# A mixture-of-experts stage whose first layer keeps the expert's weights in the array and streams the tokens, with the second layer's weights resident

## The chip, the cores and the metric

The kernel runs on one core of one Trainium2 chip. The metric is device time in microseconds (us) of one execution; the profile is one execution recorded by the hardware profiler. TensorE appears in it twice, as PE (matmuls) and PEld (weight loads), VectorE as DVE, ScalarE as ACT, GpSimd as POOL and SyncE as SP; SPq, POOLq and PEldq are the instruction queues of these engines.

## The reference

Everything is float32. A block-sparse attention over 4 batches, 8 heads, 768 positions and 64 dimensions per head gives `x` of 3072 tokens by 512. A gate picks one of 8 experts for each token, and the token goes through that expert's two layers:

```python
logits = x @ w_gate                      # 3072 x 8
expert_idx = np.argmax(logits, axis=1)
gate_w = softmax(logits)[arange, expert_idx]
for e in range(8):                       # the tokens of expert e
    h = np.maximum(x_e @ w1[e], 0.0)     # 512 -> 1024
    y_e = h @ w2[e]                      # 1024 -> 512
out = gate_w[:, None] * y
```

Each expert's `w1` is 512x1024 and its `w2` 1024x512, 2 MB either way.

## The kernel before, in words

The kernel has three stages.

**Attention** (to about 426 us): for 16 pairs of heads and two halves of the queries, scores with keys on the partitions (`scores`, L187), their exponential on ACT, the product with V (`attend`, L208), and `rows_out` (L223), which turns the result into rows of tokens, sums the exponentials and computes the gate's logits. `rows_out` issues on TensorE, back to back, six small float32 products with a moving operand of one column (L231) and three with one of 144 columns (L236); a float32 product is two weight loads and two matmuls in the trace, so that these show as 12 and 6. The rows go to a scratch tensor `x_rows` in HBM. During this stage the POOL queue loads all eight experts' `w1` into one resident tile, 16 MB (`load_w`, L92).

**Routing** (to about 460 us): DVE computes for every token its expert and its slot, so that the tokens stand sorted by expert in 31 chunks of 128 slots, a chunk having one expert only. `xe` (L458) holds the expert of each chunk; `g_idx` and `s_idx` (L495, L498) hold the rows to gather and to scatter.

**Experts** (from about 464 us): 31 chunks. For chunk i

- `gather(i)` (L510): POOL gathers 128 rows of `x_rows` by an indirect DMA into `xg` (four buffers).
- `fetch(i)` (L517): SP reads the chunk's expert from `xe` into a register and fetches that expert's `w2`, 2 MB, into one of two buffers.
- `turn_x(i)` (L522): four transposes on TensorE put the features on the partitions (`tpg`), and DVE copies them to `xgT` (two buffers).
- `layer1(i)` (L529): `xgT` is the weight operand, 128 columns at a time, and the resident `w1` streams through the array 512 columns at a time: 8 matmuls into `hp`, 128 tokens by 1024 features. DVE and ACT apply the ReLU on a half each (L540, L541) and write `h`.
- `turn_h(i)` (L543): `h` has the tokens on the partitions, so eight more transposes (`tph`) and two copies (DVE L550, ACT L552) give `hT`.
- `layer2(i)` (L554): `hT` is the weight operand and the fetched `w2` streams, 8 matmuls of 512 columns into `zp`. DVE multiplies by the gate's weight (L559) and POOL scatters the rows into the output (L560).

The loop at the end of the function writes this with layer 1 one chunk ahead of layer 2. A scheduler turns it into one instruction list per engine, each run in order, and puts the semaphores in. It also pulls reads of `xe` into registers ahead of other work. Every float32 matmul below is two weight loads and two matmuls in the trace; a transpose is one of each.

Of the kernel before, what the change touches and what calls it, by code (L numbers as in the profile page):

```python
# [8 lines left out]
F32 = mybir.dt.float32  # L9
# [3 lines left out]
AF = mybir.ActivationFunctionType  # L13
# [5 lines left out]
def kernel(  # L19
# [11 lines left out]
    nc = tc.nc  # L31
    P = 128
# [7 lines left out]
    N, DM = out.shape  # L40
    E = moe_w_gate.shape[1]
    F = moe_w1.shape[2]
    DB = DM // P
    FB = F // P
    NT = N // P
    NC = NT + E - 1
# [7 lines left out]
    big = ctx.enter_context(tc.tile_pool(name="big", bufs=1))  # L54

    ident = const.tile([P, P], F32, name="ident")
# [2 lines left out]
    nc.scalar.dma_start(wg[:], moe_w_gate.rearrange("(c p) e -> p c e", p=P))  # L59
    lgn = const.tile([P, NT, E], F32, name="lgn")  # L60
    lmax = const.tile([P, NT], F32, name="lmax")
    w1_all = big.tile([P, DB, E, F], F32, name="w1_all")

    x_d = nc.dram_tensor("x_rows", (N, XW), F32, kind="Internal").ap()

# [24 lines left out]
        loaded[(b, pr)] = got  # L90

    def load_w(e):  # L92
        nc.gpsimd.dma_start(w1_all[:, :, e, :], moe_w1[e].rearrange("(c p) f -> p c f", p=P))

    load(0, 0)

# [194 lines left out]
    for i in range(len(steps) + 2):  # L291
        if i < len(steps):
            n, half, g = steps[i]
            if half == 1 and g == 0 and n + 2 < len(pairs):
                load(*pairs[n + 2])
            if half == 0 and g == 2 and n % 2 == 0 and n // 2 < E:
                load_w(n // 2)
            for c in range(g * GR, (g + 1) * GR):
                scores(n, half, c)
        if 0 <= i - 1 < len(steps):  # L300
            n, half, g = steps[i - 1]
            for c in range(g * GR, (g + 1) * GR):
                attend(n, half, c)

        if i < len(steps) and steps[i][2] == 1:
            n, half, _ = steps[i]
            turning = turn(*pairs[n + 1], half) if n + 1 < len(pairs) else iter(())
            next(turning, None)
            if i > 3:
                rows_out(*steps[i - 2][:2])  # L310
            for _ in turning:
                pass
# [75 lines left out]
    xe = const.tile([1, NC], I32, name="xe")  # L388
# [113 lines left out]
    xp = ctx.enter_context(tc.tile_pool(name="xp", bufs=2))  # L502
    wp = ctx.enter_context(tc.tile_pool(name="wp", bufs=2))
    ps_h = ctx.enter_context(tc.tile_pool(name="ps_h", bufs=2, space=PSUM))
    ps_m = ctx.enter_context(tc.tile_pool(name="ps_m", bufs=2, space=PSUM))
    ps_z = ctx.enter_context(tc.tile_pool(name="ps_z", bufs=2, space=PSUM))
    w2v = moe_w2.rearrange("e (a p) d -> p e a d", p=P)
    st = [{} for _ in range(NC)]

    def gather(i):  # L510
        xg = st[i]["xg"] = xp.tile([P, XW], F32, name="xg", bufs=4)
        nc.gpsimd.indirect_dma_start(  # L512
            out=xg[:], out_offset=None, in_=x_d[:, :],
            in_offset=bass.IndirectOffsetOnAxis(ap=g_idx[:, i : i + 1], axis=0),
        )

    def fetch(i):  # L517
        e = nc.sync.value_load(xe[0:1, i : i + 1], min_val=0, max_val=E - 1)
        w2 = st[i]["w2"] = wp.tile([P, FB, DM], F32, name="w2")
        nc.sync.dma_start(w2[:], w2v[:, bass.ds(e, 1)].rearrange("p e a d -> p (e a) d"))  # L520

    def turn_x(i):  # L522
        tp = ps_m.tile([P, DB, P], F32, name="tpg", tag="m")
        for c in range(DB):
            nc.tensor.transpose(tp[:, c, :], st[i]["xg"][:, c * P : (c + 1) * P], ident[:])
        st[i]["xT"] = xp.tile([P, DB, P], F32, name="xgT")
        nc.vector.tensor_copy(st[i]["xT"][:], tp[:])  # L527

    def layer1(i):  # L529
        e = nc.tensor.value_load(xe[0:1, i : i + 1], min_val=0, max_val=E - 1)  # L530
        hp = ps_h.tile([P, 2, 512], F32, name="hp")
        h = st[i]["h"] = xp.tile([P, F], F32, name="h")
        for f in range(2):
            for c in range(DB):
                nc.tensor.matmul(  # L535
                    hp[:, f, :], lhsT=st[i]["xT"][:, c, :],
                    rhs=w1_all[:, c, bass.ds(e, 1), f * 512 : (f + 1) * 512].rearrange("p e f -> p (e f)"),
                    start=(c == 0), stop=(c == DB - 1),
                )
        nc.vector.tensor_relu(h[:, :512], hp[:, 0, :])  # L540
        nc.scalar.activation(h[:, 512:], hp[:, 1, :], AF.Relu)  # L541

    def turn_h(i):  # L543
        hT = st[i]["hT"] = xp.tile([P, FB, P], F32, name="hT")
        for g in range(2):
            tp = ps_m.tile([P, 4, P], F32, name="tph", tag="m")
            for m in range(4):
                nc.tensor.transpose(tp[:, m, :], st[i]["h"][:, (4 * g + m) * P : (4 * g + m + 1) * P], ident[:])  # L548
            if g == 0:
                nc.vector.tensor_copy(hT[:, :4, :], tp[:])  # L550
            else:
                nc.scalar.copy(hT[:, 4:, :], tp[:])  # L552

    def layer2(i):  # L554
        zp = ps_z.tile([P, DM], F32, name="zp")
        for fb in range(FB):
            nc.tensor.matmul(zp[:], lhsT=st[i]["hT"][:, fb, :], rhs=st[i]["w2"][:, fb, :], start=(fb == 0), stop=(fb == FB - 1))  # L557
        zo = xp.tile([P, DM], F32, name="zo")
        nc.vector.tensor_scalar(zo[:], zp[:], scalar1=st[i]["xg"][:, DM : DM + 1], scalar2=None, op0=ALU.mult)  # L559
        ins = nc.gpsimd.indirect_dma_start(  # L560
            out=out[:, :], out_offset=bass.IndirectOffsetOnAxis(ap=s_idx[:, i : i + 1], axis=0),
            in_=zo[:], in_offset=None, bounds_check=N - 1, oob_is_err=False,
        )
        ins = getattr(ins, "ins", ins)
        tc.declare_no_dep(ins, group="rows_out", reason="disjoint rows")
        tc.add_to_no_dep_group("rows_out", ins)
        st[i].clear()

    for i in range(2):
        gather(i)  # L570
        fetch(i)
    turn_x(0)
    layer1(0)
    for i in range(NC):
        if i + 2 < NC:
            gather(i + 2)
        if i + 1 < NC:
            turn_x(i + 1)
            layer1(i + 1)
        turn_h(i)  # L580
        layer2(i)
        if i + 2 < NC:
            fetch(i + 2)


# [28 lines left out]
```

## Time and profile before

| what | us |
|---|---|
| median of 3 runs | 968.87 (968.75 to 971.04) |
| the profiled execution's own time | 969.39 |
| its span, first to last instruction | 967.7 |
| attention, to the last work of L236 | about 426 |
| first matmul of layer 1 | 466.45 |
| one chunk in the loop | 15.88 |
| last scatter issued | 960.06 |

The span leaves out 1.7 us of the execution's own time. The profile's table of busy time gives each engine's share of the span; the timeline lists instructions in order of time, merged, with the start and the length of each piece; the table by stretches gives the busy time and the granted clock between two instants.

### The profile page before, as it was taken

How to read it: one execution, taken by the hardware profiler on the slowest of the kernel's cores; microseconds unless marked ns; L12 is line 12 of the kernel's file. 1: busy time of each engine (PE TensorE's matmuls, PEld its weight loads, DVE VectorE, ACT ScalarE, POOL GpSimd, SP SyncE). 2: the span in 40 equal slices, each digit the busy share in tenths (PEclk: the TensorE clock that was granted, in tenths of full speed). 3: DMA queues.
4: the chain of work that ended last, by engine and by line, in shares of the span. 5: the costliest groups of instructions: out<-in, count | busy, mean ns of one | idle time of the engine just before them, and what ended most of it. 6: DMA issues, size and time to landing. Idle time of an engine off the chain costs nothing.

```text
span 967.7 us, 10826 instructions
## 1 busy us (share of the span) xinstructions
PE 901.3 (93%) x4110; PEld 458.7 (47%) x4110; DVE 321.4 (33%) x621; ACT 221.5 (23%) x323; POOL 76.4 (8%) x103
## 2 busy tenths in 40 slices
PE   4999999999999999964799999999999999999996
PEld 2455555555555555534344444444444444444442
DVE  3555555555555555544111111111111111111111
ACT  1444444444444444420000000000000000000000
POOL 4000000000000000000111101010101010101000
PEclk9999999999999999985899999999999999999999
DMA  9982222222222210004136354544445454535350
GB/s 307 391 243 66 66 65 57 62 66 67 66 66 66 67 50 17 17 21 175 44 117 210 123 188 136 182 145 174 156 171 166 157 178 149 186 140 199 128 177 0
DMA packets 112255, 122.41 MB, mean 126 GB/s; under 512 B 56451, under 2 KB 72835, under 8 KB 112196
## 3 DMA queue, kind: packets, MB, share of 16 engines
q1 hardware_dynamic: 102484, 90.28, 30.8%
q0 software_dynamic: 9184, 31.33, 8.3%
q8 instruction: 36, 0.59, 0.2%
q14 instruction: 23, 0.19, 0.1%
q10 hardware_dynamic: 528, 0.02, 0.0%
HBM read 108.93 MB, written 14.52 MB: 128 GB/s over the span
## 4 chain that ended last, share of the span: by engine, by line
issue 47%; POOL 5%; PE 1%; DVE 1%; POOLq 0%; DVEq 0%
POOL xg L512 3%; POOL out_dram L560 1%; PE tok_ps L492 1%; DVE oh_r L487 0%; POOLq L609 0%; DVE oh_c L479 0%; DVE oh_c L483 0%; POOLq L512 0%; DVE sl L467 0%; POOLq L560 0%; DVE pr__10054 L432 0%; PE cps L437 0%; PE cps L438 0%; POOL lt_strict L409 0%; DVE xk L452 0%
## 5 line engine op out<-in xcount | busy, mean ns | idle before, releaser
L535 PE MATMUL hp<-w_all,xgT 128*128 x496 | 221.8, 600 | 16.5 <-DVE xgT L527 16.5
L557 PE MATMUL zp<-w,hT 128*128 128x512 f32 x496 | 218.2, 593 | 1.1 <-DVE hT L550 1.1
L200 ACT ACTIVATE e<-s 128x768 f32<-128x768 f32 x192 | 155.3, 811 | 94.8 <-PE s L198 93.1
L195 PE MATMUL s<-qT,kT 64*128 64x384 f32 x768 | 167.4, 514 | 0.0
L535 PEld LDWEIGHTS hp<-w_all,xgT 128*128 128x128 f32 x496 | 92.3, 191 | 128.2 <-issue 104.8
L206 DVE TENSOR_TENSOR esum<-esum,e 128x768 f32<-128x768 f32 x128 | 122.6, 958 | 71.5 <-ACT e L200 64.5
L215 PE MATMUL op<-e,v_sb 128*64 128x384 f32 x768 | 144.8, 499 | 0.0
L557 PEld LDWEIGHTS zp<-w,hT 128*128 128x128 f32 x496 | 91.8, 190 | 105.3 <-issue 103.8
L552 ACT COPY hT<-tph 128x512 f32<-128x512 f32 x31 | 18.1, 585 | 436.8 <-PE tph L548 436.8
L195 PEld LDWEIGHTS s<-qT,kT 64*128 64x128 f32 x768 | 64.1, 188 | 64.8 <-ACT e L200 38.0
L559 DVE TENSOR_SCALAR zo<-zp,xg 128x512 f32<-128x512 f32 x31 | 23.3, 751 | 204.3 <-PE zp L557 204.3
L540 DVE TENSOR_SCALAR h<-hp 128x512 f32<-128x512 f32 x31 | 21.4, 692 | 207.5 <-PE hp L535 207.5
L215 PEld LDWEIGHTS op<-e,v_sb 128*64 128x64 f32 x768 | 46.6, 136 | 80.1 <-issue 79.9
L560 POOL DMA_INDIRECT out_dram<-zo,s_idx x31 | 31.5, 1017 | 429.7 <-DVE zo L559 429.7
L198 PE MATMUL s<-pen,oh 64*128 64x384 bf16 x384 | 63.8, 326 | 0.0
L206 DVE TENSOR_TENSOR esum<-e 128x768 f32<-128x768 f32 x32 | 30.7, 958 | 68.4 <-ACT e L200 68.4
L231 PEld LDWEIGHTS xr<-ones,esum 128*128 128x128 f32 x384 | 45.4, 192 | 1.8 <-DVE esum L206 1.2
L231 PE MATMUL xr<-ones,esum 128*128 128x1 f32 x384 | 45.0, 244 | 0.0
L548 PEld LDWEIGHTS tph<-ident,h 128*128 128x128 f32 x248 | 30.0, 141 | 16.4 <-issue 16.4
L548 PE MATMUL tph<-ident,h 128*128 128x128 f32 x248 | 36.9, 273 | 0.0
L396 POOL IOTA first_w_i<- 128x8 int32 x1 | 0.1, 134 | 421.7 <-SPq L372 421.7
L512 POOL DMA_INDIRECT xg<-x_rows,g_idx x31 | 30.3, 977 | 31.9 <-issue 31.9
(116 smaller groups left out, 400.3 us busy)
## 6 DMA issues: line engine op xcount, KB each, us to landing
w<-in_moe_w_dram SPq DMA_DIRECT2D x31, 2048.0 KB, 10.3
w_all<-in_moe_w_dram POOLq DMA_DIRECT2D x8, 2048.0 KB, 32.9
k_sb<-in_k_dram SPq DMA_DIRECT2D x32, 192.0 KB, 3.7
q_sb<-in_q_dram SPq DMA_DIRECT2D x32, 192.0 KB, 3.3
v_sb<-in_v_dram SPq DMA_DIRECT2D x16, 384.0 KB, 3.3
x_rows<-xb SPq DMA_DIRECT2D x16, 384.0 KB, 3.8
xg<-x_rows,g_idx POOLq DMA_INDIRECT x31, 7.3
out_dram<-zo,s_idx POOLq DMA_INDIRECT x31, 7.7
```

The lines of the kernel that those rows point to most:

```text
L195: nc.tensor.matmul(s[:, hh, :CW], lhsT=kT[r, c * P : (c + 1) * P], rhs=qT[r, cols], start=True, stop=False)
L198: nc.tensor.matmul(s[:, hh, :CW], lhsT=oh[r, c, :], rhs=pen[r, cols], start=False, stop=True)
L200: nc.scalar.activation(e[:], s[:, :, :CW], AF.Exp, scale=scale)
L206: nc.vector.tensor_add(t[:], es[(n, half, 0)][:] if c == 1 else t[:], e[:])
L215: nc.tensor.matmul(op[hh * D : (hh + 1) * D, :], lhsT=v_sb[:, hh, c, :], rhs=e[:, hh, :], start=(c == 0), stop=(c == NCH - 1),)
L231: nc.tensor.matmul(xr[:, HC * M + 2 * m + hh : HC * M + 2 * m + hh + 1], lhsT=esum[:, hh, m * P : (m + 1) * P], rhs=ones[:], start=True, s ...
L512: nc.gpsimd.indirect_dma_start(out=xg[:], out_offset=None, in_=x_d[:, :], in_offset=bass.IndirectOffsetOnAxis(ap=g_idx[:, i : i + 1], axis=0),
L535: nc.tensor.matmul(hp[:, f, :], lhsT=st[i]["xT"][:, c, :], rhs=w1_all[:, c, bass.ds(e, 1), f * 512 : (f + 1) * 512].rearrange("p e f -> p ...
L548: nc.tensor.transpose(tp[:, m, :], st[i]["h"][:, (4 * g + m) * P : (4 * g + m + 1) * P], ident[:])
L557: nc.tensor.matmul(zp[:], lhsT=st[i]["hT"][:, fb, :], rhs=st[i]["w2"][:, fb, :], start=(fb == 0), stop=(fb == FB - 1))
L559: nc.vector.tensor_scalar(zo[:], zp[:], scalar1=st[i]["xg"][:, DM : DM + 1], scalar2=None, op0=ALU.mult)
L560: ins = nc.gpsimd.indirect_dma_start(out=out[:, :], out_offset=bass.IndirectOffsetOnAxis(ap=s_idx[:, i : i + 1], axis=0), in_=zo[:], in_of ...
```

## The change

The two layers change roles. `w2` of all experts is now the resident tile `w2_all`, and the chunk's `w1` is what SP fetches. In layer 1 a 128x128 block of `w1` is the weight operand and the chunk's 128 tokens (`xgT`) stream: 32 matmuls of 128 columns in place of 8 of 512. The result has the features on the partitions already, so `turn_h` with its eight transposes and two copies goes, and the ReLUs write `hT` directly. Layer 2 is as before except that its moving operand comes from the resident tile, at an address from a register. In the loop, `fetch` is written ahead of layer 1 where it stood behind layer 2.

```diff
-    w1_all = big.tile([P, DB, E, F], F32, name="w1_all")
+    w2_all = big.tile([P, FB, E, DM], F32, name="w2_all")
...
-        nc.gpsimd.dma_start(w1_all[:, :, e, :], moe_w1[e].rearrange("(c p) f -> p c f", p=P))
+        nc.gpsimd.dma_start(w2_all[:, :, e, :], moe_w2[e].rearrange("(a p) d -> p a d", p=P))
...
-        w2 = st[i]["w2"] = wp.tile([P, FB, DM], F32, name="w2")
-        nc.sync.dma_start(w2[:], w2v[:, bass.ds(e, 1)].rearrange("p e a d -> p (e a) d"))
+        w1 = st[i]["w1"] = wp.tile([P, DB, F], F32, name="w1")
+        nc.sync.dma_start(w1[:], w1v[:, bass.ds(e, 1)].rearrange("p e c f -> p (e c) f"))
...
     def layer1(i):
-        e = nc.tensor.value_load(xe[0:1, i : i + 1], min_val=0, max_val=E - 1)
-        hp = ps_h.tile([P, 2, 512], F32, name="hp")
-        h = st[i]["h"] = xp.tile([P, F], F32, name="h")
-        for f in range(2):
-            for c in range(DB):
-                nc.tensor.matmul(
-                    hp[:, f, :], lhsT=st[i]["xT"][:, c, :],
-                    rhs=w1_all[:, c, bass.ds(e, 1), f * 512 : (f + 1) * 512].rearrange("p e f -> p (e f)"),
-                    start=(c == 0), stop=(c == DB - 1),
-                )
-        nc.vector.tensor_relu(h[:, :512], hp[:, 0, :])
-        nc.scalar.activation(h[:, 512:], hp[:, 1, :], AF.Relu)
-
-    def turn_h(i):
         hT = st[i]["hT"] = xp.tile([P, FB, P], F32, name="hT")
         for g in range(2):
-            tp = ps_m.tile([P, 4, P], F32, name="tph", tag="m")
-            for m in range(4):
-                nc.tensor.transpose(tp[:, m, :], st[i]["h"][:, (4 * g + m) * P : (4 * g + m + 1) * P], ident[:])
+            hp = ps_h.tile([P, FB // 2, P], F32, name="hp")
+            for m in range(FB // 2):
+                fb = g * (FB // 2) + m
+                for c in range(DB):
+                    nc.tensor.matmul(
+                        hp[:, m, :], lhsT=st[i]["w1"][:, c, fb * P : (fb + 1) * P], rhs=st[i]["xT"][:, c, :],
+                        start=(c == 0), stop=(c == DB - 1),
+                    )
             if g == 0:
-                nc.vector.tensor_copy(hT[:, :4, :], tp[:])
+                nc.vector.tensor_relu(hT[:, : FB // 2, :], hp[:])
             else:
-                nc.scalar.copy(hT[:, 4:, :], tp[:])
+                nc.scalar.activation(hT[:, FB // 2 :, :], hp[:], AF.Relu)
...
     def layer2(i):
+        e = nc.tensor.value_load(xe[0:1, i : i + 1], min_val=0, max_val=E - 1)
         zp = ps_z.tile([P, DM], F32, name="zp")
         for fb in range(FB):
-            nc.tensor.matmul(zp[:], lhsT=st[i]["hT"][:, fb, :], rhs=st[i]["w2"][:, fb, :], start=(fb == 0), stop=(fb == FB - 1))
+            nc.tensor.matmul(
+                zp[:], lhsT=st[i]["hT"][:, fb, :], rhs=w2_all[:, fb, bass.ds(e, 1), :].rearrange("p e d -> p (e d)"),
+                start=(fb == 0), stop=(fb == FB - 1),
+            )
...
     for i in range(2):
-        gather(i)
         fetch(i)
+        gather(i)
...
         if i + 2 < NC:
             gather(i + 2)
+            fetch(i + 2)
         if i + 1 < NC:
             turn_x(i + 1)
             layer1(i + 1)
-        turn_h(i)
         layer2(i)
-        if i + 2 < NC:
-            fetch(i + 2)
```

On TensorE, in the middle of the loop, the list before reads as follows (`zp` is layer 2 of a chunk, `tpg` the turned tokens of the next, `tph` the turned hidden features, `hp` layer 1; ISA sets an address from a register):

```order
L557 MATMUL zp<-w_11692,hT 128x512 x8
L525 MATMUL tpg<-ident,xg 128x128 x4
L548 MATMUL tph<-ident,h 128x128 x4
L535 ISA
L535 MATMUL hp<-w_all,xgT 128x512
```

The last two rows come eight times in all; then follow the other four `tph` and the next eight `zp`. With the change the same place reads:

```order
L526 MATMUL tpg<-ident,xg 128x128 x4
L551 ISA
L551 MATMUL zp<-w_all,hT 128x512
L551 ISA
L551 MATMUL zp<-w_all,hT 128x512
L538 MATMUL hp<-xgT,w_11505 128x128 x32
L551 ISA
L551 MATMUL zp<-w_all,hT 128x512
```

The `tph` are gone, the 32 `hp` stand in one run, and two of a chunk's eight `zp` have moved between the turned tokens and layer 1, which needs them. That is so in 20 chunks; in the last 7 of the loop one `zp` stands there, behind a read of `xe`.

On SP, at the end of the routing, the list before has each of the first two fetches right behind its own read of `xe`:

```order
L518 TENSOR_LOAD xe
L518 ISA x2
L520 ISA
L520 DMA w_10155<-in_moe_w_dram 128x8x512
L518 TENSOR_LOAD xe
L518 ISA x2
L520 ISA
L520 DMA w_10168<-in_moe_w_dram 128x8x512
```

With the change 17 such reads come first, of which the last is the first row here:

```order
L519 TENSOR_LOAD xe
L519 ISA x2
L521 ISA
L521 DMA w_10153<-in_moe_w_dram 128x4x1024
L521 ISA
L521 DMA w_10166<-in_moe_w_dram 128x4x1024
```

So the first fetch has moved behind 16 further reads. The fetches bring 1024 contiguous numbers per run where they brought 512.

On TensorE, at the start of the experts, the tokens of four chunks are turned ahead of the first layer 1, where before it were two chunks (one row of `tpg`, x8), with reads of `xe` behind them:

```order
L548 ISA x2
L526 MATMUL tpg<-ident,xg 128x128 x16
L548 TENSOR_LOAD xe
L548 ISA x2
L548 TENSOR_LOAD xe
```

There are five reads behind the 16 transposes, then `hp` of chunks 0 and 1 (x32 each), `zp` of chunk 0, `hp` of chunk 2, and so on.

## Rows read from the trace of the kernel before

**Rows 1.** The page's busy time of each engine: us, share of the span, instructions.
```profile
PE 901.3 (93%) x4110; PEld 458.7 (47%) x4110; DVE 321.4 (33%) x621; ACT 221.5 (23%) x323; POOL 76.4 (8%) x103
```

**Rows 2.** Busy time by stretches: stretch, length, engines, granted clock, DMA share, GB/s.
```profile
443.00:457.00 14.00, 9.17 (x43) 9.17 (x44) 5.99 (x11) 0.00 (x0) 0.00 (x0) 0.50 0.84 299
462.00:468.00 6.00, 3.54 (x10) 2.30 (x11) 1.38 (x2) 0.00 (x0) 2.67 (x3) 0.50 0.64 178
507.17:523.05 15.88, 15.31 (x44) 7.32 (x44) 2.63 (x5) 1.08 (x2) 1.99 (x3) 1.00 0.49 163
523.05:538.93 15.88, 15.31 (x44) 7.32 (x44) 2.64 (x5) 1.08 (x2) 2.00 (x3) 1.00 0.49 167
```

**Rows 3.** Timeline of TensorE over one chunk: start, length, engine, line, instruction, count.
```profile
641.63 7.03 PE L557 MATMUL zp<-w,hT 128*128 128x512 f32 x16
648.50 0.60 PE L525 MATMUL tpg<-ident,xg 128*128 128x128 f32 x4
648.94 0.60 PE L548 MATMUL tph<-ident,h 128*128 128x128 f32 x4
650.11 7.13 PE L535 MATMUL hp<-w_all,xgT 128*128 x16 [0.57 <-DVE xgT L527]
657.08 0.60 PE L548 MATMUL tph<-ident,h 128*128 128x128 f32 x4
657.51 0.59 PE L557 MATMUL zp<-w,hT 128*128 128x512 f32 x1
```

**Rows 4.** Timeline of VectorE over the same place.
```profile
648.71 0.75 DVE L559 TENSOR_SCALAR zo<-zp,xg 128x512 f32<-128x512 f32 x1 [6.54 <-PE zp L557]
649.37 0.68 DVE L527 COPY xgT<-tpg 128x512 f32<-128x512 f32 x1
```

**Rows 5.** Timeline of matmuls and weight loads in `rows_out`; two rows cut to an instant.
```profile
416.83 1.50 PE L231 MATMUL xr<-ones,esum 128*128 128x1 f32 x12
418.19 0.98 PE L236 MATMUL xr<-mix,oT 128*128 128x144 f32 x6
...
416.83 1.42 PEld L231 LDWEIGHTS xr<-ones,esum 128*128 128x128 f32 x12 [0.60 <-DVE esum L206]
418.16 0.79 PEld L236 LDWEIGHTS xr<-mix,oT 128*128 128x128 f32 x6
...
418.40 0.53 PE L236 MATMUL xr<-mix,oT 128*128 128x144 f32 x3
...
418.89 0.29 PE L236 MATMUL xr<-mix,oT 128*128 128x144 f32 x1
```

**Rows 6.** Durations in ns (min/median/max) of weight loads in `rows_out`.
```profile
L231 PEld LDWEIGHTS xr<-ones,esum x12: 186/192/192, 416.8 to 418.1; 128*128 128x128 f32 x12
L236 PEld LDWEIGHTS xr<-mix,oT x6: 190/190/192, 418.2 to 418.8; 128*128 128x128 f32 x6
```

**Rows 7.** Timeline of TensorE: eight transposes in a row, and the routing's matmuls.
```profile
447.83 10.44 PE L492 MATMUL tok_ps<-oh_c,oh_r 128*128 128x31 f32 x48 [8.38 <-DVE oh_r L487]
...
950.26 1.04 PE L548 MATMUL tph<-ident,h 128*128 128x128 f32 x8
```

**Rows 8.** SP's reads of `xe`, durations in ns, first and last start; its first fetches.
```profile
L518 SPq TENSOR_LOAD <-xe x31: 262/262/284, 442.2 to 460.5; - x31
...
L518 SPq TENSOR_LOAD <-xe x3: 267/274/275, 444.7 to 445.9; - x3
...
L520 SPq DMA_DIRECT2D w<-in_moe_w_dram x2: 380/392/405, 443.1 to 444.3; - x2
...
DMA to landing us min/median/max: 14.1/14.1/14.1
```

**Rows 9.** Timeline of the experts' start: POOL's gathers, TensorE.
```profile
460.42 1.06 POOL L512 DMA_INDIRECT xg<-x_rows,g_idx  x1 [22.75 <-issue]
464.33 0.95 POOL L512 DMA_INDIRECT xg<-x_rows,g_idx  x1 [0.30 <-issue]
...
464.14 1.08 PE L525 MATMUL tpg<-ident,xg 128*128 128x128 f32 x4 [5.87 <-DMA xg<-x_rows,g_idx]
465.54 1.12 PE L525 MATMUL tpg<-ident,xg 128*128 128x128 f32 x4 [0.31 <-DMA xg<-x_rows,g_idx]
466.45 14.88 PE L535 MATMUL hp<-w_all,xgT 128*128 x32
```

**Rows 10.** The page's DMA issues: count, KB each, median us to landing.
```profile
w<-in_moe_w_dram SPq DMA_DIRECT2D x31, 2048.0 KB, 10.3
w_all<-in_moe_w_dram POOLq DMA_DIRECT2D x8, 2048.0 KB, 32.9
xg<-x_rows,g_idx POOLq DMA_INDIRECT x31, 7.3
```

**Rows 11.** Timeline of the end.
```profile
951.86 7.13 PE L557 MATMUL zp<-w,hT 128*128 128x512 f32 x16 [0.57 <-DVE hT L550]
...
960.06 0.98 POOL L560 DMA_INDIRECT out_dram<-zo,s_idx  x1 [7.58 <-DVE zo L559]
```

More of the change, by code (lines that the diff above doesn't have):

```diff
@@ L506 @@
     ps_z = ctx.enter_context(tc.tile_pool(name="ps_z", bufs=2, space=PSUM))
-    w2v = moe_w2.rearrange("e (a p) d -> p e a d", p=P)
+    w1v = moe_w1.rearrange("e (c p) f -> p e c f", p=P)
     st = [{} for _ in range(NC)]
@@ L569 @@
     for i in range(2):
+        fetch(i)
         gather(i)
-        fetch(i)
     turn_x(0)
```

## The prediction

> **What bounds the kernel now.** First the busy times of the page [rows 1]: TensorE works 93% of the span, every other compute engine a third or less. Then the table by stretches [rows 2]: two chunks of the expert stage, 15.88 us each, have TensorE busy 15.31 us at full granted clock, DVE 2.6 us, ACT 1.1 us and the DMA engines half their time. So a chunk costs what TensorE's list for it costs, and the timeline of TensorE over one chunk [rows 3] gives the parts by their starts: layer 2 6.87 us (641.63 to 648.50; 16 matmuls, 0.429 each), turned tokens 0.44, the first four `tph` with the wait behind them 1.17 (648.94 to 650.11), layer 1 6.97, the other four `tph` 0.43. These make 15.88. The wait is for DVE, which must finish `zo` before it copies the turned tokens [rows 4]: from the first transpose at 648.50 to layer 1 at 650.11 pass 1.61 us.
>
> **What goes.** The `tph` with the wait, 1.17 + 0.43 = 1.60 us a chunk. Two copies of `hT` go too, but DVE and ACT are idle most of the chunk [rows 2], so that is worth nothing by itself. The wait for DVE stays possible, but the list now has two `zp` (1.72 us) in 20 chunks between the turned tokens and layer 1: 0.44 + 1.72 is over 1.61, so no wait. In seven chunks only one `zp` stands there: 0.44 + 0.86 = 1.30, a wait of 0.31 each, 2.2 us in all.
>
> **What is added.** Layer 1 streams as many columns as before (8 x 512 = 32 x 128), but in 64 matmuls a chunk with a weight load each, where 16 had one each. At 0.429 us for 512 columns, 128 take 0.107; what the pair of load and matmul costs is the whole question. No row shows this pair, its neighbours do [rows 5, 6]:
>
> - 12 pairs with one moving column, so weight loads and little else: 1.42 us less the last load's 0.19, over 11 steps, 0.112 a pair.
> - 6 pairs with 144 columns: from the second matmul (418.40) to the last (418.89) 4 steps of 0.1225. The stream alone is 0.429 x 144 / 512 = 0.121. A weight load that takes about 0.11 therefore lies wholly beside the matmul ahead of it.
> - 8 transposes, 128 columns each: 1.04 less 0.27 over 7 steps, 0.110 a pair [rows 7].
> - At half the granted clock, the routing's 48 pairs with 31 columns: 10.44 less 0.40 over 47 steps, 0.214, twice the 0.107 of the load, with nothing on top for the columns [rows 2, 7].
>
> So the pair costs the longer of load and stream, 0.112 against 0.107. I take 0.112, the row nearest in its load; 0.110 and 0.1225 bound it. Layer 1 then costs 64 x 0.112 = 7.17 us a chunk, 0.20 more than its 6.97.
>
> The register addresses move from layer 1's operand to layer 2's, eight settings a chunk; layer 1 had them without a gap, so I count nothing.
>
> **The fetches.** Per chunk the bytes are the same. Written earlier, `fetch(i+2)` waits only for the buffer that layer 1 of chunk i reads, and has until layer 1 of i+2, two chunks less one layer 1: 2 x 14.5 - 7.2 = 21.8 us, against a landing of 10.3, at most 14.1 where two start together [rows 8, 10]. Gathers and scatters keep their order on POOL. SP has nothing else queued behind a waiting fetch but the next fetch. The resident load becomes 16 MB in runs half as long; an expert's lands in 32.9 us [rows 10], some 400 us ahead of its use, so I count nothing.
>
> **The start of the experts pays.** SP now does 17 reads of `xe` ahead of the first fetch. 28 steps from 444.7 to 460.5 are 0.564 us each [rows 8], so the first fetch goes out at 442.2 + 17 x 0.564 + 0.3 = 452.1 in place of 443.1. Two fetches took 14.1 us to land, so 466.2 without company; the four gathers, issued from 460.42 to 465.28 [rows 9], now share the DMA engines with them (the fetches moved 4.2 MB at 299 GB/s, the gathers 1.07 MB [rows 2]), which puts all of it at about 469. TensorE's list turns four chunks, not two, ahead of the first layer 1, so it waits for the fourth gather too, whose issue ends at 465.28 and which in any case lands 2.6 us later (as the first did: 461.48 to 464.14), 467.9. With 0.9 us for the last transposes at the low clock, and five reads of `xe` behind them (five times some 0.56 us, hidden if the queue runs ahead), layer 1 of chunk 0 starts between 468.8 and 473; I take 471, against 466.45 before.
>
> **The sum.** From there TensorE is one list: layer 1 31 x 7.17 = 222.2; layer 2 31 x 16 x 0.429 = 213.0 (rounded up by the 0.0004 that 6.87/16 has more); turned tokens 27 x 0.44 = 11.9; the waits 2.2; the edges between blocks 1.5 (half of the 0.10 that layer 1 shows before, 31 times); the low clock at the start 1.0 (32 matmuls took 14.88 where 31 x 0.429 + 0.59 = 13.9 was due [rows 3, 9]). Together 451.8, so the last `zp` ends at 922.8. The end is unchanged: from the last `zp` (951.86 + 16 x 0.429 = 958.73 [rows 11]) to the end of the span at 967.70 are 8.97 us. The span is then 931.8, the execution's own time 1.7 more, 933.5. The profiled execution, at 969.39, is 0.5 above the median of 968.87, so I predict **933.0 us** beside that median, 3.7% faster.
>
> **Where the skill speaks.** The Trainium skill, page "TensorE: Matmul & The Clock Gate", section on the back-to-back issue gap, says that in a stream of weight load and matmul pairs a 128-column matmul takes about 81 ns where the isolated one takes 56. Carried over as an estimate, these 25 ns on each of 1984 pairs of 0.107 would give 0.132 and about 973 us, no gain at all. The 144-column pairs at 0.1225, 2 ns above their stream, speak against it.
>
> **The rivals.**
>
> 1. *The pairs cost more than their longer half.* A step between streams, not seen at 512 columns because it hides there, or a TensorE queue that cannot issue 128 instructions in 7 us. The six 144-column pairs, taken from the very first (418.19 to 418.89, 5 steps), cost 0.14 each, since the first stands 0.21 ahead of the second. If every pair paid that, 1984 x 0.028 = 56 us more: 989 us, slower. It decides at a pair of 0.130, where 1984 x 0.018 eats the whole gain. Against it: the four even steps. If only each of the eight chains of eight matmuls paid 0.1 us once, 25 us: 958, still faster.
> 2. *Load and stream run one after the other* because each load must wait for the array to be free of the matmul ahead. A pair is then 0.112 + 0.107 = 0.22 and the time 933 + 1984 x 0.107 = 1145 us. Against it speak both the 144-column steps and the 48 routing pairs. The same page of the Trainium skill, in its part on row and column tiling, says that a load overlaps matmuls in flight only where it targets other rows of the array; all loads here use all rows, so by that rule this is the case. The trace disagrees, at 0.1225 a pair.
> 3. *The weights come late.* If the first fetch, or the gathers beside it, takes longer than reckoned, the start moves by up to 10 us: 943. If fetches took over 21.8 us in the loop, every chunk would wait; the longest shown is 14.1.
>
> **How the numbers follow.** A measurement of this kernel tells a change of about 0.3%, some 3 us, from none. The forecast, pairs between 0.110 and 0.1225 and a start between 468.8 and 473, spans 933 - 4 - 2 - 1.5 = 925 to 933 + 21 + 2 = 956; I give it 0.89, rival 3 within it. A pair at the bare 0.107 would save 10, 923: 0.03 for that or less. Rival 1 has 0.05, with 0.02 of it near no change; rival 2 0.03. Faster 0.92, same 0.02, slower 0.06. The upper end, with every pair as slow as one of 144 columns, is the least likely part of the forecast, so the range is 922 to 952.
>
> **What would show it.** Right: layer 1 of a chunk in one run of 64 matmuls over 7.0 to 7.4 us, no idle time between two blocks in most chunks, a chunk of 14.5 us, a first layer 1 near 471 at 452 for the first fetch, TensorE still at full granted clock. Wrong: a pair of 0.13 or more in the timeline of layer 1; gaps ahead of `hp` that end with a DMA; a granted clock below 1 in the loop.

## The result, and the profile after

The changed kernel takes 935.79 us (median of 4 runs, 933.29 to 943.27) against 968.83 of the kernel before in the same series: a ratio of 0.967, 95% interval 0.961 to 0.973. The prediction was 933.0 in a range of 922 to 952.

The execution shown here took 937.63 us, its span is 935.9. The page's busy times, to set beside [rows 1]:

```profile
PE 881.2 (94%) x5350; PEld 562.5 (60%) x5350; DVE 303.1 (32%) x590; ACT 206.4 (22%) x292; POOL 78.0 (8%) x103
```

TensorE has 1240 matmuls more and is busy 20 us less. The timeline of TensorE over two chunks of the loop (start, length, engine, line, instruction, count), which answers to [rows 3]:

```profile
646.64 0.60 PE L526 MATMUL tpg<-ident,xg 128*128 128x128 f32 x4
647.08 1.88 PE L551 MATMUL zp<-w_all,hT 128*128 x4
648.80 7.31 PE L538 MATMUL hp<-xgT,w 128*128 128x128 f32 x64
655.94 5.32 PE L551 MATMUL zp<-w_all,hT 128*128 x12
661.09 0.60 PE L526 MATMUL tpg<-ident,xg 128*128 128x128 f32 x4
```

A chunk lasts 14.45 us (646.64 to 661.09) instead of 15.88, and no row shows idle time ahead of it. Layer 1 takes 7.14 us from its start to that of the next block, 0.1116 us for each of the 64 pairs of weight load and matmul; layer 2 keeps 0.429 a matmul. In a chunk with only one `zp` ahead of layer 1 the wait for the turned tokens is there:

```profile
894.39 0.60 PE L526 MATMUL tpg<-ident,xg 128*128 128x128 f32 x4
894.82 1.02 PE L551 MATMUL zp<-w_all,hT 128*128 x2
895.99 7.41 PE L538 MATMUL hp<-xgT,w 128*128 128x128 f32 x64
```

The one `zp` (two matmuls) takes 0.86 us from 894.82, so TensorE is free for layer 1 at 895.68; it starts at 895.99, 0.31 later. The stretches (length, PE, PEld, DVE, ACT, POOL, granted clock, DMA share, GB/s) show TensorE without a gap at full clock; beside it the DMA engines are half idle, as in [rows 2]:

```profile
600.00:700.00 100.00, 100.00 (x587) 73.51 (x586) 14.27 (x21) 4.04 (x7) 13.96 (x14) 1.00 0.51 180
700.00:800.00 100.00, 100.00 (x583) 73.19 (x582) 14.27 (x21) 3.73 (x7) 13.96 (x14) 1.00 0.52 184
```

The start of the experts is another matter. TensorE, to set beside [rows 7, 9] (`issue` marks idle time in which the engine waited for nothing that the profile shows):

```profile
451.39 10.44 PE L492 MATMUL tok_ps<-oh_c,oh_r 128*128 128x31 f32 x48 [8.38 <-DVE oh_r L487]
470.65 1.08 PE L526 MATMUL tpg<-ident,xg 128*128 128x128 f32 x4 [8.82 <-DMA xg<-x_rows,g_idx]
...
475.34 1.09 PE L526 MATMUL tpg<-ident,xg 128*128 128x128 f32 x4 [0.81 <-DMA xg<-x_rows,g_idx]
478.91 13.36 PE L538 MATMUL hp<-xgT,w 128*128 128x128 f32 x92 [2.49 <-issue]
```

The routing's matmuls stand 3.56 us later than before, and from them to the first layer 1 pass 27.5 us where before it was 18.6. SP's instructions of the fetch's line (durations in ns, first and last start), the wait that ends among them (us in total, times, longest) and the landing of the first two fetches show what held them:

```profile
L521 SPq EVENT_SEMAPHORE  x35: 17/17/6946, 455.5 to 874.2; - x35
L521 SPq FUSED_REGOPS  x31: 37/37/48, 455.4 to 874.1; - x31
L521 SPq MOVE w<-in_moe_w_dram x31: 29/29/39, 462.8 to 874.2; - x31
...
SPq L521 <- DVE s_idx L498: 7.0, 1, 7.0
...
DMA to landing us min/median/max: 15.4/15.4/15.4
```

SP had its 17 reads behind it at 455.4 and then stood 6.9 us waiting for the routing's last instruction on DVE (`s_idx`, L498); the first fetch went out at 462.8 and landed 15.4 us later, at 478.2, where layer 1 starts at 478.91. The page's DMA issues (KB each, median us to landing), beside [rows 10]:

```profile
w<-in_moe_w_dram SPq DMA_DIRECT2D x31, 2048.0 KB, 7.8
w_all<-in_moe_w_dram POOLq DMA_DIRECT2D x8, 2048.0 KB, 31.0
...
xg<-x_rows,g_idx POOLq DMA_INDIRECT x31, 3.4
```

The sum of the profiled execution: from the first layer 1 to the last scatter it has 453.30 us (478.91 to 932.21) instead of 493.61, 40.3 less; the start is 12.5 later (478.91 against 466.45); behind the last scatter the span goes on 3.69 us instead of 7.64, 4.0 less. Together 31.8, which is 967.7 less 935.9.

### The profile page after: what moved, and what is told of

The parts are those of the page before. It is cut to its first block, busy times and chain, and to the rows that moved or that the text cites. A ratio compares the mean times of both kernels' runs of the same rounds, so it can differ in the third digit from the quotient of the medians.

```text
span 935.9 us, 13135 instructions
## 1 busy us (share of the span) xinstructions
PE 881.2 (94%) x5350; PEld 562.5 (60%) x5350; DVE 303.1 (32%) x590; ACT 206.4 (22%) x292; POOL 78.0 (8%) x103
## 4 chain that ended last, share of the span: by engine, by line
issue 46%; POOL 5%; PE 1%; DVE 1%; POOLq 0%; DVEq 0%
POOL xg L512 3%; POOL out_dram L557 1%; PE tok_ps L492 1%; DVE oh_r L487 0%; POOLq L604 0%; DVE oh_c L479 0%; DVE oh_c L483 0%; DVE sl L467 0%; POOLq L512 0%; POOLq L557 0%; DVE pr__10054 L432 0%; PE cps L437 0%; PE cps L438 0%; POOL lt_strict L409 0%; DVE xk L452 0%
## 5 line engine op out<-in xcount | busy, mean ns | idle before, releaser
L538 PEld LDWEIGHTS hp<-xgT,w 128*128 128x128 f32 x1984 | 228.4, 194 | 20.2 <-DVE xgT L528 11.6
L538 PE MATMUL hp<-xgT,w 128*128 128x128 f32 x1984 | 230.0, 277 | 3.5 <-issue 2.5
L551 PE MATMUL zp<-w_all,hT 128*128 x496 | 222.3, 592 | 0.0
L551 PEld LDWEIGHTS zp<-w_all,hT 128*128 128x128 f32 x496 | 89.8, 190 | 91.3 <-issue 91.3
L545 ACT ACTIVATE hT<-hp 128x512 f32<-128x512 f32 x31 | 18.5, 597 | 468.3 <-PE hp L538 461.8
L543 DVE TENSOR_SCALAR hT<-hp 128x512 f32<-128x512 f32 x31 | 21.4, 691 | 137.3 <-issue 117.0
L198 PEld LDWEIGHTS <-oh 64*128 64x128 bf16 x384 | 19.6, 95 | 25.6 <-issue 1.7
L526 PEld LDWEIGHTS tpg<-ident,xg 128*128 128x128 f32 x124 | 16.4, 151 | 25.7 <-issue 25.0
```

Of the source, the lines that this page charges most:

```text
L198: nc.tensor.matmul(s[:, hh, :CW], lhsT=oh[r, c, :], rhs=pen[r, cols], start=False, stop=True)
L538: nc.tensor.matmul(hp[:, m, :], lhsT=st[i]["w1"][:, c, fb * P : (fb + 1) * P], rhs=st[i]["xT"][:, c, :], start=(c == 0), stop=(c == DB - 1),)
L543: nc.vector.tensor_relu(hT[:, : FB // 2, :], hp[:])
L551: nc.tensor.matmul(zp[:], lhsT=st[i]["hT"][:, fb, :], rhs=w2_all[:, fb, bass.ds(e, 1), :].rearrange("p e d -> p (e d)"), start=(fb == 0), ...
```

## The experiments

In the loop the question was what a pair of load and stream costs and what the transposes and their wait were worth; ahead of it, why the start was late; and behind it, why the end was early. The kernel before had medians of 969.6, 969.8 and 969.7 us in the three series, so that times can be set side by side.

### Layer 1 in 64 columns

```diff
-                for c in range(DB):
-                    nc.tensor.matmul(
-                        hp[:, m, :], lhsT=st[i]["w1"][:, c, fb * P : (fb + 1) * P], rhs=st[i]["xT"][:, c, :],
...
+                for t in range(2):
+                    cols = slice(t * P // 2, (t + 1) * P // 2)
+                    for c in range(DB):
+                        nc.tensor.matmul(
+                            hp[:, m, cols], lhsT=st[i]["w1"][:, c, fb * P : (fb + 1) * P], rhs=st[i]["xT"][:, c, cols],
...
```

> The changed kernel with layer 1's moving tile halved: 64 token columns stream through each weight tile, twice, so a chunk has 128 float32 pairs of a 128-column weight load and a 64-column matmul instead of 64 pairs of 128 columns. Theory, that the weight load sets a pair's pace (0.1116 us each in the changed kernel's trace, whatever streams beside it): layer 1 takes 128 x 0.112 = 14.3 us a chunk, 7.15 more, times 31 chunks = 222 us, so about 1158 us. Rival A, that the stream sets it (0.107 for 128 columns, half of that for 64): a pair takes about 0.056, layer 1 stays at 7.1 us and the time at about 936. Rival B, that load and stream run one after the other (0.11 and half a stream): about 0.165 a pair, 21 us a chunk, about 1370 us.

Measured: 1184.64 us (one run). TensorE's timeline in the loop:

```profile
716.83 14.40 PE L540 MATMUL hp<-xgT,w 128*128 128x64 f32 x128
731.06 5.37 PE L553 MATMUL zp<-w_all,hT 128*128 x12
```

128 pairs take 14.23 us, 0.1112 each: with half the stream a pair costs what it did. The weight load sets the pace, and both rivals fall. The total is 27 us above the theory's 1158, and 25 of them are the clock. TensorE at the experts' start:

```profile
479.23 54.84 PE L540 MATMUL hp<-xgT,w 128*128 128x64 f32 x256 [2.48 <-issue]
533.86 9.05 PE L553 MATMUL zp<-w_all,hT 128*128 x16
542.75 14.40 PE L540 MATMUL hp<-xgT,w 128*128 128x64 f32 x128
```

and the stretches there (the last number but two is the granted clock):

```profile
480.00:500.00 20.00, 20.00 (x96) 20.00 (x95) 0.69 (x1) 0.00 (x0) 0.00 (x0) 0.50 0.00 1
500.00:520.00 20.00, 20.00 (x96) 20.00 (x95) 0.69 (x1) 0.60 (x1) 0.00 (x0) 0.50 0.29 106
...
538.00:540.00 2.00, 2.00 (x6) 0.95 (x5) 0.00 (x0) 0.00 (x0) 0.00 (x0) 1.00 1.01 418
```

The first 256 pairs ran at a granted clock of 0.50 (1.2 GHz), 54.6 us instead of 28.5, though by the profile TensorE was never idle; the clock rose some 4 us after the first layer 2 had begun. With that layer 2 (8.89 instead of 6.87) it is 28.2 us, 25 more than the 2.9 that the low clock costs the changed kernel. 31 x 7.09 and these 25 make 245 of the 247 by which the spans differ.

### No turning of the hidden features

```diff
-            nc.tensor.matmul(zp[:], lhsT=st[i]["hT"][:, fb, :], rhs=st[i]["w2"][:, fb, :], start=(fb == 0), stop=(fb == FB - 1))
+            nc.tensor.matmul(zp[:], lhsT=st[i]["h"][:, fb * P : (fb + 1) * P], rhs=st[i]["w2"][:, fb, :], start=(fb == 0), stop=(fb == FB - 1))
...
-        turn_h(i)
```

> The kernel before without the turning of the hidden features: the 8 transposes a chunk and their two copies are left out, and the second layer takes the untransposed tile as its weight operand, so it multiplies other numbers in the same shapes. Wide streams of the first layer and everything else stay. Theory, that the change's gain per chunk is the transposes with their wait (1.6 to 1.7 us) less the dearer first layer (0.3 us more): this kernel keeps the first and doesn't pay the second, chunk about 14.2 us instead of 15.9, 29 chunks x 1.7 = 49 us, about 919 us. Rival, that the wait on the copies only moves (the second layer then waits for the sigmoid-side work that made the tile): a chunk keeps 0.5 us of it, about 934. Rival, that the stage is bound by the weights' transfers: no change, 969.

Measured: 925.57 us (one run). The loop:

```profile
649.74 7.03 PE L535 MATMUL hp<-w_all,xgT 128*128 x16
656.61 5.31 PE L557 MATMUL zp<-w,h 128*128 128x512 f32 x12
661.76 0.60 PE L525 MATMUL tpg<-ident,xg 128*128 128x128 f32 x4
662.20 1.88 PE L557 MATMUL zp<-w,h 128*128 128x512 f32 x4
663.92 7.03 PE L535 MATMUL hp<-w_all,xgT 128*128 x16
```

A chunk is 14.18 us, as the theory has it, and the wait is gone, not moved (the expectation's "sigmoid-side work" is the two ReLUs). That is the gain without its price: 1.70 a chunk, of which the changed kernel keeps 1.43 (15.88 to 14.45). The total is 6 to 7 us above the theory. From the first layer 1 to the last scatter it saves 46.7, where I had counted 29 chunks at 1.7, 49.3; and its first layer 1 starts at 469.20, 2.75 later than before. Here too SP's first fetch stood behind 17 reads and then 7.0 us behind L498; it went out at 458.94 instead of 443.1 [rows 8], and beside the gathers, which took 7.2 us to land instead of 3.7. This kernel has lost a tile of the same size as the changed one (`hT` instead of `h`); the run on the weights' buffers below says why that matters.

### Token transposes one chunk earlier

```diff
+    gather(2)
...
+    turn_x(1)
...
+        if i + 3 < NC:
+            gather(i + 3)
         if i + 2 < NC:
-            gather(i + 2)
+            turn_x(i + 2)
         if i + 1 < NC:
-            turn_x(i + 1)
             layer1(i + 1)
```

> The kernel before, complete, with the token gather and its transpose one chunk further ahead, so that the token transposes' copy and the first layer of a chunk no longer meet: TensorE has the eight matmuls of the second layer between the token transpose and the first layer that needs it. Transposes of the hidden features stay. Theory, that of the 1.6 us a chunk that the change removes about 0.6 to 0.8 were waits and 0.9 the transposes' own time: chunk about 15.06 instead of 15.9, 29 chunks, about 944 to 947 us. Rival, that covering the waits gives all that the change gave: about 936. Rival, that the waits only move to the next copy: within 3 us of 969.

Measured: 945.71 us (median of 5, 945.07 to 951.16), ratio 0.975, 95% interval 0.973 to 0.977. The loop:

```profile
639.51 7.03 PE L557 MATMUL zp<-w,hT 128*128 128x512 f32 x16
646.38 0.60 PE L525 MATMUL tpg<-ident,xg 128*128 128x128 f32 x4
646.81 6.17 PE L535 MATMUL hp<-w_all,xgT 128*128 x14
652.82 1.04 PE L548 MATMUL tph<-ident,h 128*128 128x128 f32 x8
653.70 1.02 PE L535 MATMUL hp<-w_all,xgT 128*128 x2
654.56 7.03 PE L557 MATMUL zp<-w,hT 128*128 128x512 f32 x16
```

15.05 us a chunk, with all eight transposes still in it (0.88 from their start to the next block) and no wait. So 0.83 of a chunk's 15.88 was waiting and its edges, of the 1.43 by which the change shortens it. The total gains 24 us by writing the gather and the transposes of the tokens a chunk earlier, against the change's 33; but those 33 are net of a start that came late, and with that mended (below) the change gains 44, of which 4 are POOL's shorter drain. The rest needs the transposes to go.

### Resident rows of 2 KB in the kernel before

```diff
-        nc.gpsimd.dma_start(w1_all[:, :, e, :], moe_w1[e].rearrange("(c p) f -> p c f", p=P))
+        for f in range(2):
+            nc.gpsimd.dma_start(
+                w1_all[:, :, e, f * 512 : (f + 1) * 512], moe_w1[e, :, f * 512 : (f + 1) * 512].rearrange("(c p) f -> p c f", p=P),
+            )
```

> The kernel before with each resident load of first-layer weights at its start split into two halves of 512 columns, so that its rows are 2 KB long, as the changed kernel's second-layer rows are, and not 4 KB. Nothing else. Theory, that the shorter rows are what made the changed kernel's attention end 3.5 us later (the third k pair arrives late beside the load): the routing starts at about 438.5 instead of 434.9, the load takes until past 65 us, and the time is about 972. Rival, that the row length doesn't matter and the later end came from the order or the number of buffers: within 1 us of 968.8, routing at 435.

Measured: 965.57 us (median of 4, 965.34 to 965.74), ratio 0.996, 95% interval 0.994 to 0.997. Both answers were wrong. The attention is not late (the last block of `rows_out` starts at 425.20; before, 425.01), so the row length does not delay it. But the kernel is 4 us faster, small but clear of the noise by the interval, and the gain lies behind the last scatter, issued at 960.25 (before 960.06): POOL's long drain, an instruction at the kernel's end, shrinks. Its row (ns min/median/max) in the kernel before:

```profile
L609 POOLq DRAIN  x3: 51/109/7010, 959.8 to 967.4; - x3
```

in this one:

```profile
L612 POOLq DRAIN  x3: 51/109/2957, 960.0 to 963.7; - x3
```

and in the changed kernel:

```profile
L604 POOLq DRAIN  x3: 51/109/2942, 932.0 to 935.6; - x3
```

The last scatter lands 2.1 us after its issue in all three.

### Twice the loads, rows of 4 KB

```diff
-        nc.gpsimd.dma_start(w1_all[:, :, e, :], moe_w1[e].rearrange("(c p) f -> p c f", p=P))
+        for half in range(2):
+            c0 = half * DB // 2
+            nc.gpsimd.dma_start(
+                w1_all[:, c0 : c0 + DB // 2, e, :],
+                moe_w1[e, c0 * P : (c0 + DB // 2) * P, :].rearrange("(c p) f -> p c f", p=P),
+            )
```

> The kernel before with each resident load split in two halves of 256 rows, so that its rows keep 4 KB and only the number of loads on POOL's queue doubles (16 instead of 8). The run with halves of 512 columns (16 loads, 2 KB rows) ended with a drain of POOL of 2.96 us instead of 7.01 and was 4 us faster, with the same last scatter. Theory, that the row length of the resident load decides POOL's drain at the end: here it stays at 7.0 us and the time at about 969. Rival, that the number of loads decides: the drain is 2.95 us and the time about 965.5.

Measured: 969.87 us (median of 10, 968.62 to 973.69), ratio 1.0005, 95% interval 0.9996 to 1.0015.

```profile
L614 POOLq DRAIN  x3: 51/109/7663, 959.4 to 967.6; - x3
```

The drain stays long, so it goes with the row length of loads that landed some 900 us earlier, not with their number; all eleven traces sort so (seven with rows of 2 KB, four with rows of 4 KB). What the drain waits for no run shows.

### The resident load spread over the attention

```diff
             if half == 0 and g == 2 and n % 2 == 0 and n // 2 < E:
+                nc.gpsimd.tensor_copy(w2_all[0:1, 0, n // 2, 0:1], es[(n, 0, 0)][0:1, 0, 0:1])
                 load_w(n // 2)
```

> The changed kernel with its resident load spread: before the load of each expert's second-layer weights POOL copies one element of an exponential tile of the attention into that expert's place, so that the load can't start before the attention has come so far. Theory, that the resident load beside the first k and q pairs costs the changed kernel's attention its 3.5 us (a wait of 2.1 us on k and slower issues): the wait on k goes, the routing starts at or below 435 instead of 438.5, the time is 3.5 us or more below the changed kernel's, about 932 against 935.8, and its runs lie closer together. Rival, that the load later in the attention collides with the k and q pairs as much as at its start: routing at 438 or later, no change. Rival, that POOL's copies hold up the attention's own POOL work: slower by some us.

Measured: 933.54 us (median of 6, 932.58 to 934.57), ratio 0.961, 95% interval 0.956 to 0.966.

### The changed kernel again

No edit.

> The changed kernel itself, with nothing altered, beside the kernel before. Theory, that the resident load beside the first k and q pairs makes its attention end early or late by chance: its runs spread over 5 us or more, from about 932 to 943, where those with the spread load kept within 2 us, and their median is 934 to 937. Rival, that the spread of its first four runs came from the chip they ran on: within 2 us around one value.

Measured: 935.08 us (median of 5, 933.75 to 941.26), ratio 0.966, 95% interval 0.964 to 0.969.

The spread is the changed kernel's own: its nine runs reach from 933.3 to 943.3, those with the spread load stay within 2.0 us. In the trace first shown, the waits of TensorE on DMA (us in total, times, longest) between 15 and 100 us are in the changed kernel

```profile
PE tp L176 <- DMA k_sb<-in_k_dram: 2.1, 1, 2.1
```

and in the kernel with the tokens turned earlier, whose attention and resident load are those of the kernel before,

```profile
PE tp L176 <- DMA k_sb<-in_k_dram: 3.5, 1, 3.5
```

with the granted clock at 0.97 and 0.93 between 20 and 70 us, and the attention's last block 3.5 and 6.3 us later than before. With the load spread the wait is 0.6, the clock 1.00, and that block starts at 424.79. The execution of the changed kernel profiled in this series had no such wait, and its last block starts at 424.24. So the delay strikes some executions and not others, with rows of 2 KB or of 4, and with the load spread it is not seen. I read it as a collision of the early resident load with the first k pairs; no trace shows the collision itself, and why four of the changed kernel's nine runs lie above 937 us, where of the 37 of the kernel before only two stand out (981.05 and 981.96), stays open. The spread load is worth 1.5 to 2.3 us in the median (against 935.08 and 935.79), less than the 3.5 expected and below the 3 us by which a measurement tells a change from none; the narrow spread of its runs says more.

### The weights' buffers clear of the routing's memory

The tile `h` is gone, so the pool ahead of the weights' buffers is 8 KB per partition smaller and these have moved. By the sizes of the tiles in the two kernels, that pool took 32,896 bytes of a partition and now takes 24,704; it lies where the routing's pool of 24,860 bytes lay. So the first weights' buffer now covers the last 156 bytes of the routing's pool, in `tv` and `none`, which L498 reads; where it lay before, it was clear of them. An unused pool of 8 KB puts the buffers back:

```diff
+    gap = ctx.enter_context(tc.tile_pool(name="gap", bufs=1))
+    gap.tile([P, 2 * F], F32, name="gap")
```

> The changed kernel with an 8 KB pool that nothing uses between the transposed tokens' pool and the weights' buffers, so that these lie where they lay before, clear of the routing's memory. Theory, that the first fetch of weights stood 6.9 us behind the routing's last work only because the buffers overlapped it, and that the five reads of expert numbers fell into the first layer for the same reason: the first fetch is issued within 1 us of its own read, at about 456, the first layer 1 starts some 5 to 8 us earlier than 478.9, and the time is 5 to 8 us below the changed kernel's, about 928 to 931. Rival, that the token gathers (their end at 467) set the start and the weights were not last: about 2 us at most. Rival, that what is gained at the start is lost to a longer low clock: within 1 us.

Measured: 926.23 us (median of 6, 925.66 to 929.23), ratio 0.953, 95% interval 0.948 to 0.958; 9 us below the changed kernel's 935.1 to 935.8. SP's fetches and TensorE's start:

```profile
L523 SPq MOVE w<-in_moe_w_dram x31: 29/29/38, 445.7 to 865.6; - x31
```

```profile
450.51 10.45 PE L492 MATMUL tok_ps<-oh_c,oh_r 128*128 128x31 f32 x48 [8.35 <-DVE oh_r L487]
466.25 1.08 PE L528 MATMUL tpg<-ident,xg 128*128 128x128 f32 x4 [5.29 <-DMA xg<-x_rows,g_idx]
467.55 1.12 PE L528 MATMUL tpg<-ident,xg 128*128 128x128 f32 x4 [0.22 <-DMA xg<-x_rows,g_idx]
468.46 16.28 PE L540 MATMUL hp<-xgT,w 128*128 128x128 f32 x128
```

The first fetch goes out at 445.8, 17 us earlier: the wait for L498 is gone, and the fetch stands behind one read, not 17. The gathers no longer meet it, two chunks' tokens are turned ahead of layer 1 and not four, and no read stands between. From the routing's matmuls to layer 1 it is 17.95 us instead of 27.5. That is more than the 5 to 8 us expected, which left the 17 reads ahead of the fetch. So the late start was the place of a buffer: overlapping the routing's memory, the weights had to wait for the routing's last work, and with the overlap the scheduler's list changes too. How the 9 us divide between the fetch and the rest of the list this run does not show; in the changed kernel the first weights landed at 478.2, 0.7 us ahead of layer 1, so that the five reads on TensorE can have cost 0.7 at most.

### Both

> The changed kernel with both edits, the spread resident load and the 8 KB gap. Theory: the two act in different stages and add up, 3.5 and 5 to 8 us, about 924 to 927 us. Rival, that the resident load, spread, or the earlier fetch reach into each other's stage: less than the sum of the two alone by over 2 us.

The changed kernel with the spread load and the gap. Measured: 925.60 us (median of 6, 924.90 to 926.70), ratio 0.953, 95% interval 0.948 to 0.958. The edits add up within 1 us (8.9 and 1.5 alone, 9.5 together, against 935.08). This is the fastest complete version: 10 us below the changed kernel, 44 below the kernel before.

## Why the prediction was right, and where its terms were off

The cause was right and is shown: no transposes and hardly a wait, at a pair that costs its weight load. The start and the end were wrong, in opposite directions. The span had been put at 931.8 and is 935.9; by steps:

- **The pair.** Taken as 0.112, it is 0.1116, and it stays 0.1112 with half the stream. Rivals 1 and 2 (0.13 or more, 0.22) fall, and so does the step of 25 ns a pair that the prediction had weighed (0.132). The Trainium skill's sentence behind rival 2, on the page "TensorE: Matmul & The Clock Gate", in the part on row and column tiling, that a load overlaps only where it targets other rows, does not hold here: all loads use all rows, and with 0.107 of stream beside it a pair takes the same 0.11 as with half of that.
- **What goes.** 1.60 a chunk of transposes and wait. The run without them shows 1.70, the difference being the 0.10 edge that layer 1 had behind its wait. The changed kernel has such an edge only in the seven chunks with a wait (layer 1 takes 7.25 there, not 7.14), 0.8 us in all where I had put 1.5.
- **The waits.** None in 20 chunks and 0.31 in the seven others, as reckoned.
- **Register addresses.** Counted as nothing, and no idle time stands at them.
- **The list from the first layer 1 to the last `zp`.** 452.07 (478.91 to 930.98) against 451.8, though not by the right parts: the low clock cost 2.9 (17.2 us for 128 pairs instead of 14.28), not 1.0, and the pair (0.8) and the edges (0.7) give most of that back.
- **The first fetch.** The failed step. The sentence that "the first fetch goes out at 442.2 + 17 x 0.564 + 0.3 = 452.1" took the reads for all that held it. They did end there (455.4, with a routing that began 3.55 later), but the fetch then waited 6.9 us for the routing's last instruction, because its buffer had moved into the routing's memory, and went out at 462.8. Why the scheduler had put the reads first I did not ask. Beside the gathers, the fourth of which ended TensorE's wait only at 475.34, the first weights landed at 478.2, 5.7 us later than the 469 taken once the late routing is off. The five reads behind the transposes, taken as hidden, end at 478.7 and can have cost 0.7 at most. Relative to the routing, layer 1 of chunk 0 came 4.4 us later than the 471 taken, at 475.4, outside the 468.8 to 473 allowed. That is rival 3 in part, by a cause that it does not name.
- **The resident load.** "I count nothing" holds for the row length, which moved no attention in the run of 2 KB rows; but in this execution the attention ended 3.54 us later, as far as the runs tell by the load beside the first k pairs, and the routing began 3.55 later.
- **The end.** "The end is unchanged" was wrong by 4.05: from the last `zp` 4.92 us, not 8.97, because the resident rows became 2 KB and the drain shorter.

3.55 + 4.4 + 0.3 - 4.05 = 4.2, the 4.1 by which the span missed, within the digits. Two unforeseen terms hid each other, the late fetch and the shorter drain, so that the total came within 3 us of the forecast in part by luck: had the drain stayed long, the median would have been near 940.

## What to carry to other kernels

A float32 layer whose result has to be turned can swap its operands instead: with 128 columns the weight load sets the pair's pace and the swap costs 2% of the layer here, while it saves every transpose and the waits that come with the copies. But first try whether the waits go by issuing the transposes a chunk earlier; that alone gave 24 us here, where the swap with its buffers in place gives 44. When a tile is deleted, look where the buffers behind it move: an overlap with memory that a previous stage still uses, here of 156 bytes, is a wait that no line of the diff shows, and it was worth 9 us.

## What the runs showed of the hardware unexpectedly

- POOL's drain at the end took 2.94 to 2.96 us where the resident loads had rows of 2 KB and 7.01 to 7.66 where they had 4 KB, with the same last scatter.
- The chunk's 2 MB of weights landed in 7.8 us in rows of 4 KB and in 10.3 in rows of 2 KB; the gathers beside them landed in 3.4 instead of 7.3 [rows 10]. The two kernels also order fetch and gather differently, and no run changes the fetch's row length alone.
- In the run with 64 columns the granted clock stayed at 0.50 (1.2 GHz) for 55 us of unbroken pairs and reached 1.00 (2.4 GHz) some 4 us after 512-column streams began. With 128 columns it rose 6 us after layer 1 began (0.56 between 484 and 485 us, 1.00 from there).
